# Gate columns carried by the V product, masks and a small product on array groups, and a new order of issue in an attention, gated MLP and expert kernel

## The chip, the cores and the metric

The kernel runs on one core of one Trainium2 chip. The core has a matrix engine (TensorE, PE in the profile; its weight loads are PEld), a vector engine (DVE), a scalar engine (ACT), GpSimd (POOL) and a queue engine (SP) that issues most transfers. Each takes its instructions strictly in the order in which they were written for it, and waits on semaphores for the others. The metric is the time of one execution on the device, in microseconds (us), the median of several runs.

## The reference, cut to what matters

Three stages follow each other, on B=2 sequences of S=768 tokens, 8 heads of 64, so 512 columns a token.

```python
# 1 attention: each chunk of 32 queries sees 8 memory keys and keys c_start-16 .. c_end+8
a = softmax(scale * q_c @ k_full.T);  x = a @ v_full            # -> x (B, S, 512)
# 2 gated MLP
h = gelu(x @ w_in)                                              # 512 -> 1024
u, v = h[..., :512], h[..., 512:]
v_s = einsum('ts,bsd->btd', w_sg, layernorm(v) * g_ln) + b_sg[None, :, None]
x = x + (u * v_s) @ w_out
# 3 experts: 8 of them, one for each token
logits = x @ w_gate;  local = sigmoid(x @ w_local)
e[s] = argmax(logits[s]) if s == 0 or local[s] < 0.5 else e[s-1]
out[s] = softmax(logits[s])[e] * (relu(x[s] @ w1[e]) @ w2[e])   # 512 -> 1024 -> 512
```

## The kernel before, in words

Tokens are worked in 12 tiles of 128 (6 a sequence, `TT`). A product that needs float32 accuracy is made of three passes over operands split into a high and a low part (`PASS`: high x high, high x low, low x high); the split is one ACT or DVE copy (the `_h` tile) and one DVE subtraction (the `_l` tile). The weights `w_in` and `w_out` arrive as 64-bit floats and are rebuilt as float32 on DVE and ACT before their split (class `Conv64`).

For each tile: `Score.mm` makes the scores of 8 heads in two PSUM tiles (`sc`, 4 x 96 columns), each begun by a mask product of all 128 rows that writes all 384 columns (L390); `Attn` takes maximum, exponential and transposes (`nm`, `a`, `at`); `Head` multiplies by v and normalises (`xp`, `rs`, `xt`); `Turn` transposes to `x_h`, `x_l` (`xtp`). `V.s0` (L557) is x times the v half of `w_in`: 12 matmuls of 512 columns into a PSUM tile `vps`; its gelu is ACT Square, DVE, ACT tanh, DVE (`sq`, `th`, `vg`, L538 to L546), then layer norm to `vh`. `U` (L604) is the same with the u half. A gate g multiplies `vh` by `w_sg` (`vsp`, L633) and by `u` and splits to `g_h`, `g_l`. `X1` (L1074) adds g times `w_out` to x and writes the tile to DRAM.

The 16 logits columns (8 experts, local gate, padding) are computed without waiting for the new x: `Logits.x0` (L701, tile `lps`) multiplies the attention's x by the gate weights (`rtxa`, `rtxb`, filled by `rt_fill`, L690 to L692), 48 matmuls of 256 columns for all tokens; `Logits.g0` multiplies g by (w_out times gate weights), a small product that `ConvOut.s4` makes (`wops`, L297). `route1` and what follows make the routing, on small tiles, mostly on DVE; they end with the gathers of the first expert tile (`xg`).

The expert stage (`Moe.run`) takes tiles of 128 tokens of one expert, gathered by GpSimd: `hp` (L1204, L1227), relu to `ht`, `op` (L1268, L1280), scaling on ACT (`o`, L1291) and a scatter by GpSimd (L1292). Its last unit is a pair of tiles that share an expert.

The order is written out by hand. `ORDER` is a table of names; each issues the next piece of its work, and the engines' queues follow from the table (`v04.0`: first stage of V, sequence 0, tile 4; `t011`: transposes; `x12m0`: a quarter of an X1 product; `cv1.1`: conversion of a quarter of the v weights; R and r names: routing; `lx01.0`: logits of x; `lg01.0`: logits of g). PSUM is one pool of 8 banks, most SBUF tiles come from 94 slots of 128 x 512 floats.

Of the kernel before, what the change touches and what calls it, by code (L numbers as in the profile page):

```python
# [25 lines left out]
NE = 8  # L26
NM = 8
# [15 lines left out]
NSLOT = 94  # L43
# [16 lines left out]
t020 lu0 a150.0 cv2.1 p041 s13 t011 q14 lu1 cv2.1 cv2.1 p001 cv2.1 p011 p010 p010 a150.0 p011 p100 a110.2 p011  # L60
a110.2 cv2.1 lu2 t020 t021 p011 cu0.0 t000 p100 p001 cv1.3 lv151 p001 s14 t000 t000 lv101 p100 p100 cu1.0
cv2.2 cv2.3 t001 t001 lv121 t001 cu1.0 cu1.1 a131.0 a140.0 t021 t021 v00.0 cu1.1 a141.0 a150.2 v00.0 cu0.0
p101 v04.0 cu1.1 p101 v00.1 p101 a141.0 a140.0 p101 v00.1 a140.0 a150.2 a131.0 consts2 v00.1 v00.1 v00.1 v03.0
lv131 a141.0 v04.0 lv111 v04.1 lu3 cu3.0 v01.0 a131.0 a140.2 rx lx01.0 cu3.0 v04.1 v04.1 cu1.1 cu2.0 v03.0
cu1.1 v01.0 lx01.1 p121 v01.1 v04.1 v04.1 p111 a140.2 p111 lv110 p110 p111 lx02.0 v00.1 p111 ls8 cu2.0 cu2.1
p110 p121 v01.1 p110 ls6 v00.1 a141.2 a141.2 lo1 v03.1 v03.1 v04.1 lx02.1 a130.0 p110 cu2.1 lv130 a130.0 lv140
v05.0 t100 p121 cu2.1 cs6.0 p121 a130.0 cu3.1 lx00.0 v01.1 t100 a131.2 cu0.1 cu0.1 cu3.1 v04.1 a131.2 v03.1
cu0.1 cu2.1 cu3.1 a130.2 cu1.1 a151.2 ls2 ls0 t101 t100 a130.2 cu0.1 cu1.2 cu1.3 lv120 a151.2 v02.0 lo3 lv141
p120 p131 p130 cu3.1 cu3.1 cu3.1 v04.2 cs2.0 p151 p120 t101 cs8.0 t101 p131 v05.0 p120 p120 cu0.1 p140 lx00.1
v02.0 cu3.2 p141 p131 v01.1 co3.0 cu0.1 cu2.1 cu2.1 cu2.2 cu0.2 p151 ls1 v01.1 v11.0 lv150 p151 v01.1 co3.0  # L70
p151 p141 p131 p130 cu2.3 cs1.0 p130 v01.1 v04.2 v02.1 cu0.3 v11.0 p141 v05.1 cu3.3 p141 v02.1 p130 ls5 cs5.0
# [12 lines left out]
g02.1 g02.1 g02.1 v12.1 co0.2 g03.1 v10.1 v13.1 co2.3 co2.3 v12.1 u11.0 v14.0 v14.0 v12.1 v12.1 u10.0 v12.1
v10.2 v15.0 v15.1 v12.1 v15.1 v15.1 v15.1 u15.0 u15.0 u15.0 v13.1 co0.3 u10.1 v12.1 u15.1 u12.0 x03h0 v13.1
v15.1 u10.1 lx11.0 v14.1 v14.1 co0.4 u11.1 u11.1 v15.1 u15.1 v14.1 v12.2 v10.2 v13.1 u12.0 co0.4 v14.1 u12.0
co3.4 g01.1 u11.1 v14.1 lx11.1 u15.1 x03h1 x03.1 co3.4 v14.1 v14.1 v15.1 v14.2 u10.1 u13.0 u14.0 u14.0 co1.4
co1.4 v13.1 v13.1 v13.1 u14.0 g00.1 u14.1 u12.1 v11.2 u13.0 v13.2 v10.2 x01h0 v14.2 v13.2 u12.1 v15.2 co2.4
co2.4 v15.2 v14.2 x01h1 v12.2 v12.2 v15.2 v11.2 v13.2 lg00.0 u13.0 u13.1 lg02.0 u14.1 u12.1 lg01.0 g12h0 g12h0
g14h0 g12.1 lg01.1 g13h0 g12h1 g13h0 g12h1 lg00.1 lg02.1 r0 g13.1 r0 g14h0 g13h1 u14.1 r0 r1 g12.1 lx12.0  # L90
g14.1 g14h1 r1 r1 r1 r1 r1 g15h0 g15h0 g12.1 g10h0 lx12.1 g10h0 g10.1 r2 g15.1 g14h1 r2 g13h1 g10h1 g10h1
g13.1 r1 g14.1 g15.1 g15.1 g15h1 g10.1 g10.1 x01.1 g15.1 g11h0 g11h0 g14.1 g12.1 zero r4 r5 r5 g14.1 r5 r5 r5
r6 u13.1 u13.1 r6 x03.2 r5 g11h1 g11h1 g10.1 g11.1 g10.1 r2 g15h1 x04h0 x04h1 r6 x02h0 g12.1 g15.1 g15.1 r6 r6
g11.1 g13.1 pre0 pre1 g15.1 r6 g15.1 g13.1 x11m0 pre2 g14.1 g13.1 g11.1 x12m0 x12m1 x11m1 g11.1 g11.1 r7 r1
lg11.0 r5 x04.1 lg10.0 lg10.1 lg11.1 r5 r5 lg12.0 lg12.1 r3 x01.2 r6 x11m2 R1 x02h1 x11m3 R1 R1 R2 R2 R2 R2 R2
R2 pre3 cm0 cm1 x02.1 x05h0 x05h1 x05.1 R3 R3 x10m0 R3 RM RP RP RP RP RP RP RP x12m2 x05.2 x12m3 RA RA x13m0
x13m1 x13m2 RP x13m3 x11.1 x11.2 x10m1 RA RA RA RA RA RA x00h0 x12.1 x13.1 x10m2 x10m3 x00h1 RA RP RP RP RP RP
RA RA x10.1 x15m0 RA RZ x00.1 RP x02.2 x15m1 RP RP RP RP RP RZ R2 RP x12.2 x13.2 RL RP x14m0 x14m1 x15m2 x04.2
x10.2 RP RP RP RP x00.2 R2 x14m2 R4 x14m3 RP RP x14.1 G0 x14.2 RS RT RE RE g15.1 x15m3 x15.1 RT XL RT RT RT
x15.2 XL RS RO cm2 cm3 RP G1 XL XL G2  # L100
# [18 lines left out]
def tile_kernel(  # L119
# [21 lines left out]
    pp = ctx.enter_context(tc.tile_pool(name="pp", bufs=8, space=bass.MemoryType.PSUM))  # L141
# [7 lines left out]


# [8 lines left out]
    mind = [cp.tile([128, 128], BF16, name=f"mind{u}") for u in range(2)]  # L159

    def masks():

        n = 3 * W
        mf = slot([4, n + 128], F32, "amask_f")
        nc.sync.dma_start(mf, amask)
        nc.vector.memset(mrow, 0.0)
        nc.vector.tensor_copy(mrow[:4, :n], mf[:, :n])
        for u in range(2):
            nc.vector.memset(mind[u], 0.0)
            nc.vector.tensor_copy(  # L170
                mind[u][:4].rearrange("p (h q) -> p h q", h=2),
                mf[:, n + 64 * u : n + 64 * u + 64].unsqueeze(1).to_broadcast([4, 2, UQ]),
            )
# [37 lines left out]
    class Conv64:  # L211


        def __init__(self, raws, name, put, n):
            self.raws, self.name, self.put, self.n = raws, name, put, n
# [31 lines left out]
        def s2(self):  # L247
            self.hl = new_split(self.name)
            split_hi(self.hl[0], self.wf, ENG["CH"][self.n])

        def s3(self):
            split_lo(self.hl[1], self.wf, self.hl[0])
            self.put(self.hl)
# [13 lines left out]
    def conv_w_in(raws, kk, half):  # L267
        def put(hl):
            (win_u if half == 0 else win_v)[kk] = hl

        return Conv64(raws, f"in{kk}{half}", put, kk + 4 * (1 - half))

    wgx = cp.tile([128, NP, 16], F32, name="wgx")
    def load_w_out(f):
        return load64(w_out[f * 128 : (f + 1) * 128], 0, f"out{f}")
# [1369 lines left out]
```

## Time and profile before

| what | value |
|---|---|
| median of 3 runs | 422.45 us (421.6 to 423.23) |
| profiled execution | 422.23 us, of which span 420.5 us |
| granted TensorE clock, mean | 0.993 |
| PE / PEld busy | 398.8 us (95%) / 346.9 us (82%) |
| DVE / ACT / POOL busy | 313.6 (75%) / 190.7 (45%) / 43.9 us (10%) |
| memory traffic | 75.95 MB, mean 181 GB/s |

The span is what the profiler saw, 1.7 us less than the execution. Records of matmuls overlap, since they are pipelined and their ends are modelled: what a matmul costs on a full PE is the distance from its start to the next start, not the length of its record. The same holds, less strongly, for DVE and ACT. A stretch in which PE is 10.00 us busy of 10 is one in which it had always something to do.

### The profile page before, as it was taken

How to read it: one execution, taken by the hardware profiler on the slowest of the kernel's cores; microseconds unless marked ns; L12 is line 12 of the kernel's file. 1: busy time of each engine (PE TensorE's matmuls, PEld its weight loads, DVE VectorE, ACT ScalarE, POOL GpSimd, SP SyncE). 2: the span in 40 equal slices, each digit the busy share in tenths (PEclk: the TensorE clock that was granted, in tenths of full speed). 3: DMA queues.
4: the chain of work that ended last, by engine and by line, in shares of the span. 5: the costliest groups of instructions: out<-in, count | busy, mean ns of one | idle time of the engine just before them, and what ended most of it. 6: DMA issues, size and time to landing. Idle time of an engine off the chain costs nothing. (4 is left out here: it accounts for less than half of the span.)

```text
span 420.5 us, 9218 instructions
## 1 busy us (share of the span) xinstructions
PE 398.8 (95%) x3359; PEld 346.9 (82%) x3359; DVE 313.6 (75%) x776; ACT 190.7 (45%) x422; POOL 43.9 (10%) x61
## 2 busy tenths in 40 slices
PE   5799999999999999999999789999999999999991
PEld 3577788899999899999878669989888968958981
DVE  2999989999997988657989997986696455166430
ACT  4898677634331453011030457736484263263420
POOL 1001001030000011000000233000130120110001
PEclk9999999999999999999999999999999999999997
DMA  7999992220100000000565599999699899810001
GB/s 221 372 376 365 311 346 53 77 76 2 51 2 2 0 2 0 2 2 27 172 252 202 169 358 386 393 349 365 180 364 303 299 312 396 311 35 27 20 3 42
DMA packets 43694, 75.95 MB, mean 181 GB/s; under 512 B 5921, under 2 KB 12969, under 8 KB 43642
## 3 DMA queue, kind: packets, MB, share of 16 engines
q1 hardware_dynamic: 39674, 65.40, 45.3%
q0 software_dynamic: 2240, 6.75, 4.4%
q10 hardware_dynamic: 1728, 3.15, 2.0%
q8 instruction: 28, 0.46, 0.5%
q14 instruction: 24, 0.20, 0.1%
HBM read 68.98 MB, written 6.75 MB: 180 GB/s over the span
## 5 line engine op out<-in xcount | busy, mean ns | idle before, releaser
L192 DVE TENSOR_TENSOR we_l<-raw,we_h 128x512 fp32r<-128x512 f32 x128 | 81.1, 688 | 2.1 <-ACT o L1291 0.7
L187 ACT ACTIVATE we_h<-raw 128x512 fp32r<-128x512 f32 x105 | 58.4, 629 | 6.3 <-DVE x L1084 6.3
L1204 PE MATMUL hp<-xe_h,we_h 128*128 128x256 f32 x160 | 45.3, 283 | 0.0
L1204 PE MATMUL hp<-xe_h,we_l 128*128 128x256 f32 x160 | 44.9, 281 | 0.0
L1204 PE MATMUL hp<-xe_l,we_h 128*128 128x256 f32 x160 | 44.8, 280 | 0.0
L1280 PE MATMUL op<-we_h,ht_l 128*128 128x512 f32 x104 | 41.1, 395 | 1.3 <-DVE ht_l L192 1.3
L1280 PE MATMUL op<-we_h,ht_h 128*128 128x512 f32 x104 | 41.7, 401 | 0.1
L1280 PE MATMUL op<-we_l,ht_h 128*128 128x512 f32 x104 | 41.1, 395 | 0.2 <-DVE we_l L192 0.2
L633 PE MATMUL vsp<-sg_h,vh_h 128*128 128x256 f32 x144 | 41.1, 285 | 0.0
L633 PE MATMUL vsp<-sg_l,vh_h 128*128 128x256 f32 x144 | 40.5, 281 | 0.0
L633 PE MATMUL vsp<-sg_h,vh_l 128*128 128x256 f32 x144 | 40.4, 281 | 0.0
L1236 DVE SCALAR_TENSOR_TENSOR ht_l<-hp,ht_h 128x512 fp32r<-128x512 f32 x20 | 13.7, 688 | 28.2 <-ACT ht_h L1235 28.2
L1204 PEld LDWEIGHTS hp<-xe_h,we_h 128*128 128x128 f32 x160 | 30.2, 189 | 0.1
L1204 PEld LDWEIGHTS hp<-xe_l,we_h 128*128 128x128 f32 x160 | 30.1, 188 | 0.0
L1204 PEld LDWEIGHTS hp<-xe_h,we_l 128*128 128x128 f32 x160 | 30.1, 188 | 0.0
L1292 POOL DMA_INDIRECT out_dram<-o,sidx x15 | 15.2, 1011 | 121.9 <-ACT o L1291 102.0
L633 PEld LDWEIGHTS vsp<-sg_h,vh_h 128*128 128x128 f32 x144 | 27.1, 188 | 0.3
L604 PE MATMUL ups<-x_h,in_h 128*128 128x256 f32 x96 | 27.3, 284 | 0.0
L633 PEld LDWEIGHTS vsp<-sg_h,vh_l 128*128 128x128 f32 x144 | 27.1, 188 | 0.0
L633 PEld LDWEIGHTS vsp<-sg_l,vh_h 128*128 128x128 f32 x144 | 27.1, 188 | 0.0
L604 PE MATMUL ups<-x_h,in_l 128*128 128x256 f32 x96 | 27.0, 281 | 0.0
L604 PE MATMUL ups<-x_l,in_h 128*128 128x256 f32 x96 | 26.9, 281 | 0.0
(281 smaller groups left out, 965.7 us busy)
## 6 DMA issues: line engine op xcount, KB each, us to landing
raw<-in_w SPq DMA_DIRECT2D x160, 256.0 KB
v<-in_vw SPq DMA_DIRECT2D x23, 260.0 KB
k<-in_kw SPq DMA_DIRECT2D x24, 192.0 KB
raw_in<-in_w_in SPq DMA_DIRECT2D x16, 256.0 KB
q<-in_qT SPq DMA_DIRECT2D x12, 256.0 KB
x1d<-x ACTq DMA_DIRECT2D x12, 256.0 KB
rsg<-in_w_sgT SPq DMA_DIRECT2D x9, 256.0 KB
raw_out<-in_w_out SPq DMA_DIRECT2D x8, 256.0 KB
```

The source lines that it names most:

```text
L187: nc.scalar.activation(hi, src, AF.Copy)
L192: nc.vector.tensor_tensor(lo, src, hi.bitcast(F32), ALU.subtract)
L604: nc.tensor.matmul(ps[:, i * 256 : (i + 1) * 256], win_u[k][wa][:, f * 128 : (f + 1) * 128], xT[self.b].at(wb, k, 256 * self.g, 256), star ...
L633: nc.tensor.matmul(self.ps[:, h * 256 : (h + 1) * 256], self.vh[s].hl[wa][:, f * 128 : (f + 1) * 128], rhs_sg(wb, s, self.g), start=(s == ...
L1204: nc.tensor.matmul(ps[:, i * 256 : (i + 1) * 256], self.w[f // 4 * 4 + k][wa][:, f % 4 * 128 : (f % 4 + 1) * 128], self.x[k // 2][wb][:, k ...
L1236: nc.vector.scalar_tensor_tensor(l, self.ps[s], 0.0, h.bitcast(F32), ALU.max, ALU.subtract)
L1280: nc.tensor.matmul(self.po[c], h[wa][:, o : o + 128], self.w[8 + k][wb], start=(k == 0 and n == 0), stop=(k == 7 and n == 2),)
L1292: nc.gpsimd.indirect_dma_start(dst, bass.IndirectOffsetOnAxis(ap=sidx[:, c : c + 1], axis=0), o, None, bounds_check=NT * 512 // n - 1, oob ...
```

## The change

- **V carries the gate columns.** The split v weights become 528 wide (8 tiles of a new pool `wv`, the slots fall from 94 to 86); the last 16 columns are the split gate weights (`wide_x`, 8 small DVE instructions). Each of the 12 matmuls of a V becomes two, of 256 and 272 columns, into a PSUM tile of two banks that exists once (`vp`; the other banks fall from 8 to 6). ACT copies the 16 logits columns to `lg`. The 48 matmuls `lps` of x with their ACT copies and DVE fills are gone.
- **w_gate.** The product of w_out and the gate weights has the gate weights (32 columns) stationary and 128 columns moving, on the four column groups of the array, all in one place, with a copy and a transposition behind it.
- **Masks.** The mask product stands behind the scores, uses 4 rows (in the row groups 0 and 32) instead of 128 and writes 64 of each 96 columns.
- **Logits to routing.** DVE adds the two parts in place; two ACT copies go.
- **Last pair.** The second product of the last unit goes tile by tile, and tile 0 is scaled and scattered while tile 1 is multiplied.
- **Order.** The table is new: attention starts with tile 2; the first V stands after fewer tiles' attention; V and U alternate; all gates follow, then the logits of g, all 12 X1 tiles but for their order, and the routing of both sequences.

PE around V. First before, the border between the second and the third V (`vps_1104`, `vps_1166`), with the buffers' numbers:

```order
L557 MATMUL vps_1104<-in31_h_434,x021_h_1066 128x512
L557 MATMUL vps_1104<-in31_l_435,x021_h_1066 128x512
L557 MATMUL vps_1104<-in31_h_434,x021_l_1067 128x512
L557 MATMUL vps_1166<-in01_h_663,x010_h_712 128x512
L557 MATMUL vps_1166<-in01_l_664,x010_h_712 128x512
L557 MATMUL vps_1166<-in01_h_663,x010_l_713 128x512
```

and now, from the end of the second V (`vps_1103`) on, on the same engine:

```order
L599 MATMUL vps_1103<-in31_h_823,x021_l_1057 128x256
L599 MATMUL vps_1103<-in31_h_823,x021_l_1057 128x272
L467 MATMUL at_1137<-ident_79,a141_1049 96x128 x4
L467 MATMUL at_1148<-ident_79,a131_970 96x128 x4
L523 MATMUL xtp_1162<-ident_79,xt02_820 128x128 x2
L523 MATMUL xtp_1162<-ident_79,xt03_1004 128x128 x2
L467 MATMUL at_1172<-ident_79,a151_732 96x128 x4
L467 MATMUL at_1185<-ident_79,a130_1084 96x128 x4
L523 MATMUL xtp_1195<-ident_79,xt02_820 128x128 x2
L523 MATMUL xtp_1195<-ident_79,xt03_1004 128x128 x2
L467 MATMUL at_1203<-ident_79,a100_588 96x128 x4
L494 MATMUL xp_1217<-v110_1101,at110_933 64x65
```

Before, the third V followed the second at once, into another bank. Now transposes of attention weights (`at`) and of x (`xtp`), and eight `xp` that are not shown, stand between the second and the third V.

DVE at the first V. First before (the first two `x_l` are the two halves of the columns of tiles 0 and 1, which the first V waits for; `xt` is the normalised x, `in_l` a split weight):

```order
L192 TENSOR_TENSOR in_l<-w_in_670,in_h 128x512
L465 TENSOR_TENSOR xt_776<-xp,rs 128x256
L192 TENSOR_TENSOR x_l<-xtp,x_h 128x512
L462 RECIPROCAL rs<-rs 128x4
L465 TENSOR_TENSOR xt_977<-xp,rs 128x256
L192 TENSOR_TENSOR in_l<-w_in_827,in_h 128x512
L192 TENSOR_TENSOR x_l<-xtp,x_h 128x512
L233 TENSOR_SCALAR cv_in_1040<-cv_in_1040 128x512
L415 TENSOR_REDUCE nm<-sc 128x4 x2
L192 TENSOR_TENSOR x_l<-xtp,x_h 128x512
```

and now, around the two gelu steps of the first V (`sq`, `vg`):

```order
L582 SCALAR_TENSOR_TENSOR sq<-sq,vps 128x512
L241 TENSOR_SCALAR cv_in_939<-cv_in_939 128x512
L200 TENSOR_TENSOR x_l<-xtp,x_h 128x512
L502 TENSOR_SCALAR rs<-xp 128x4
L587 SCALAR_TENSOR_TENSOR vg<-th,vps 128x512
L457 TENSOR_REDUCE nm<-sc 128x4
L243 TENSOR_SCALAR w_in_1012<-cv_in_939 128x512
L502 TENSOR_SCALAR rs<-xp 128x4
L457 TENSOR_REDUCE nm<-sc 128x4
L200 TENSOR_TENSOR x_l<-xtp,x_h 128x512
L504 RECIPROCAL rs<-rs 128x4
L457 TENSOR_REDUCE nm<-sc 128x4
```

Before, no gelu step stood among DVE's conversions and attention work up to there; now both steps of the first V stand between the splits of x, the normalisation (`rs`) and the maxima (`nm`).

PE at the logits of g. First before, sequence 0, between X1 products, behind the last of the four small products:

```order
L1074 MATMUL x1p<-out_l,g_h 128x512
L1074 MATMUL x1p<-out_h,g_l 128x512
L297 MATMUL wops<-wgx,woTout_2444 128x16 x4
L1074 MATMUL x1p<-out_h,g_h 128x512
L1074 MATMUL x1p<-out_l,g_h 128x512
L1074 MATMUL x1p<-out_h,g_l 128x512
L1074 MATMUL x1p<-out_h,g_h 128x512
L1074 MATMUL x1p<-out_l,g_h 128x512
L1074 MATMUL x1p<-out_h,g_l 128x512
L701 MATMUL lps<-g_h,rtga 128x256
```

and now the small product, between two gate products (the first of its 16 rows):

```order
L678 MATMUL vsp<-sg_l,vh_h 128x256
L678 MATMUL vsp<-sg_h,vh_l 128x256
L319 MATMUL wops<-woTout_2791,wgx 32x128
L319 MATMUL wops<-woTout_2942,wgx 32x128
L319 MATMUL wops<-woTout_2852,wgx 32x128
```

and, behind some more gate products, the logits of sequence 0, behind the last gate product:

```order
L678 MATMUL vsp<-sg_h,vh_h 128x256
L678 MATMUL vsp<-sg_l,vh_h 128x256
L678 MATMUL vsp<-sg_h,vh_l 128x256
L735 MATMUL lps<-g_h,rta 128x256
L735 MATMUL lps<-g_l,rtb 128x256
```

The small product went from four places to one, and the logits of sequence 0 went behind the gates of both sequences.

The core of the diff:

```diff
-NSLOT = 94
+NSLOT = 86
+NWV = 8
+DL = 16
 ORDER = """
-masks lq03 q03 lq02 q02 s03 a031.0 a031.0 a031.0 lq01 a030.0 q01 lv3 s02 a021.0 a030.0 a020.0 lq04 a030.0 s01
+lq02 masks lq01 q02 s02 consts1 a021.0 q01 s01 a021.0 a021.0 a021.2 a020.0 a020.0 a020.0 a020.2 lq04 q04 s04
...
-    pp = ctx.enter_context(tc.tile_pool(name="pp", bufs=8, space=bass.MemoryType.PSUM))
+    wv = ctx.enter_context(tc.tile_pool(name="wv", bufs=NWV))
+    pp = ctx.enter_context(tc.tile_pool(name="pp", bufs=6, space=bass.MemoryType.PSUM))
+    vp = ctx.enter_context(tc.tile_pool(name="vp", bufs=1, space=bass.MemoryType.PSUM))
...
+    def bank2(name):
+        return vp.tile([128, 1024], F32, tag="d", name=name)
+    def wide(name):
+        return [wv.tile([128, 512 + DL], F32R, tag="w", name=f"{name}_{x}") for x in "hl"]
...
+    def wide_x(k):
+        h, l = (t[:, 512:] for t in win_v[k])
+        nc.vector.tensor_copy(h, wgx[:, k, :DL])
+        nc.vector.tensor_tensor(l, wgx[:, k, :DL], h.bitcast(F32), ALU.subtract)
...
-            for c in range(4):
-                nc.tensor.matmul(ps, self.t[:, c, :], wgx[:, c, :], start=(c == 0), stop=(c == 3))
-            yield
-            rt_fill("g", self.f, ps)
+    def w_gate():
+        ps = bank([128, 128], "wops")
+        for c in range(4):
+            for f in range(4):
+                nc.tensor.matmul(
+                    ps[32 * f : 32 * f + 32], wgx[:, c, :], turned[f][:, c, :], start=(c == 0), stop=(c == 3)
+                )
...
-            for u in range(2):
-                nc.tensor.matmul(
-                    self.sc[u], mind[u], mrow[:, v * W : (v + 1) * W].unsqueeze(1).to_broadcast([128, 4, W]),
-                    start=True, stop=False,
-                )
...
+            for u in range(2):
+                p = slice(32 * u, 32 * u + 4)
+                nc.tensor.matmul(
+                    part(self.sc[u]),
+                    mind[p], part(mrow[p, v * W : (v + 1) * W].unsqueeze(1).to_broadcast([4, 4, W])),
+                    start=False, stop=True,
+                )
...
         def s0(self):
-            ps = bank([128, 512], "vps")
+            ps = bank2("vps")
...
-                    nc.tensor.matmul(
-                        ps, xT[self.b].at(wa, k, self.tt * 128, 128), win_v[k][wb],
-                        start=(n == 0), stop=(n == 11),
-                    )
+                    for o0, o1 in ((0, 256), (256, 512 + DL)):
+                        nc.tensor.matmul(
+                            ps[:, 256 + o0 : 256 + o1],
+                            xT[self.b].at(wa, k, self.tt * 128, 128), win_v[k][wb][:, o0:o1],
+                            start=(n == 0), stop=(n == 11),
+                        )
...
             self.g = Gelu()
-            self.g.s0(ps)
+            self.g.s0(ps[:, 256:768])
+            yield
+            nc.scalar.activation(lg[:, self.b * TT + self.tt, :], ps[:, 768 : 768 + DL], AF.Copy)
...
-        def x0(self, i):
-            self.ps[i] = bank([128, 256], "lps")
-            logits_mm(self.ps[i], "x", xT[self.b], 256 * i, 256)
...
-        lo = tp.tile([128, TT, 16], F32, tag="r_lo", name="r_lo")
-        nc.scalar.copy(lo, ps[:, :, 16:32])
+        nc.vector.tensor_tensor(L, ps[:, :, 16:32], L, ALU.add)
         yield
-        nc.vector.tensor_tensor(L, ps[:, :, 0:16], lo, ALU.add)
+        nc.vector.tensor_tensor(L, ps[:, :, 0:16], L, ALU.add)
...
-                h, l = self.ht[s] = new_split("ht")
+                h, l = self.ht[s] = wide_split("ht")
...
             half, i = divmod(s, len(self.cols))
+            if self.last:
+                i, half = divmod(s, 2)
...
                         o.l2(s)
+                        if o.last and s == 1:
+                            o.out(0)
...
-            outs(T[-1])
+            if T[-1].last:
+                T[-1].out(1)
+            else:
+                outs(T[-1])
```

## Rows read from the trace of the kernel before

**Rows 1.** Windows of 10 us: busy us and instructions of each engine, clock, DMA, GB/s.

```profile
20.00:30.00 10.00, 8.93 (x167) 7.06 (x165) 9.79 (x30) 9.76 (x36) 0.00 (x0) 1.00 1.06 377
...
40.00:50.00 10.00, 9.49 (x149) 7.64 (x149) 9.72 (x30) 7.15 (x17) 0.00 (x0) 1.00 1.03 300
...
100.00:110.00 10.00, 10.00 (x87) 10.00 (x86) 9.44 (x21) 2.24 (x5) 0.00 (x0) 1.00 0.14 44
...
230.00:240.00 10.00, 7.83 (x67) 6.39 (x66) 9.59 (x43) 3.13 (x7) 1.43 (x2) 1.00 0.40 133
240.00:250.00 10.00, 8.68 (x41) 6.83 (x42) 9.90 (x17) 6.59 (x13) 5.16 (x5) 1.00 0.96 332
```

**Rows 2.** Timeline of PE, 45 to 48 us: start, us, line, operation, names.

```profile
45.60 0.49 PE L390 MATMUL sc<-mrow,mind 128*128 128x384 bf16 x2
46.02 0.89 PE L398 MATMUL sc<-k,q 64*64 64x96 f32 x32
...
47.26 0.48 PE L557 MATMUL vps<-in_h,x_h 128*128 128x512 f32 x1
...
48.04 0.40 PE L557 MATMUL vps<-in_h,x_h 128*128 128x512 f32 x1
48.27 0.39 PE L557 MATMUL vps<-in_l,x_h 128*128 128x512 f32 x1
```

**Rows 3.** The tile lps: duration min/median/max in ns, first and last start.

```profile
L701 PE MATMUL lps<-x_h,rtxa x24: 274/280/386, 60.1 to 182.4; 128*128 128x256 f32 x24
```

**Rows 4.** Timeline of PE around the small product wops and around a column-group product.

```profile
161.65 0.96 PE L297 MATMUL wops<-wgx,woTout 128*128 128x16 f32 x8
162.46 0.36 PE L604 MATMUL ups<-x_h,in_h 128*128 128x256 f32 x1
...
398.50 1.96 PE L1268 MATMUL op<-raw,ht 128*32 128x128 f32 x64
400.39 0.50 PE L1280 MATMUL op<-we_h,ht_h 128*128 128x512 f32 x1
```

**Rows 5.** Timeline of DVE, 45 to 58 us: start, us, line, operation, names.

```profile
45.88 0.42 DVE L465 TENSOR_TENSOR xt<-xp,rs 128x256 f32<-128x256 f32 x1
...
49.64 0.55 DVE L415 TENSOR_REDUCE nm<-sc 128x4 f32<-128x384 f32 x1
50.10 0.68 DVE L192 TENSOR_TENSOR x_l<-xtp,x_h 128x512 fp32r<-128x512 f32 x1
50.70 0.41 DVE L235 TENSOR_SCALAR w_in<-cv_in 128x512 uint32<-128x512 uint32 x1
51.03 0.55 DVE L415 TENSOR_REDUCE nm<-sc 128x4 f32<-128x384 f32 x1
...
54.55 0.67 DVE L546 SCALAR_TENSOR_TENSOR vg<-th,vps 128x512 f32<-128x512 f32 x1
...
57.02 0.17 DVE L690 CAST rtxa<-wgx 128x16 fp32r<-128x16 f32 x1
...
57.39 0.17 DVE L690 CAST rtxa<-wgx 128x16 fp32r<-128x16 f32 x1
```

**Rows 6.** Timeline of ACT at the first V's gelu.

```profile
50.33 0.60 ACT L538 ACTIVATE sq<-vps 128x512 f32<-128x512 f32 x1 [1.33 <-PE vps L557]
```

**Rows 7.** Waits of PE behind the gates: us in total, times, longest.

```profile
PE hp L1227 <- ACT xe_h L187: 1.3, 1, 1.3
...
PE inv L976 <- DVE s_eqj L957: 0.8, 1, 0.8
```

**Rows 8.** Timeline of POOL at the end.

```profile
409.99 0.98 POOL L1292 DMA_INDIRECT out_dram<-o,sidx  x1 [7.67 <-ACT o L1291]
413.48 0.98 POOL L1292 DMA_INDIRECT out_dram<-o,sidx  x1 [2.51 <-ACT o L1291]
```

**Rows 9.** Timeline of ACT at the end.

```profile
409.03 0.69 ACT L1291 ACTIVATE o<-op,psl 128x512 f32<-128x512 f32 x1 [8.00 <-PE op L1280]
411.87 0.69 ACT L1291 ACTIVATE o<-op,psl 128x512 f32<-128x512 f32 x1 [2.15 <-PEq L1557]
```

More of the change, by code (lines that the diff above doesn't have):

```diff
@@ L211, in tile_kernel, with __init__ @@
     class Conv64:
-        def __init__(self, raws, name, put, n):
-            self.raws, self.name, self.put, self.n = raws, name, put, n
+        def __init__(self, raws, name, put, n, new=None):
+            self.raws, self.name, self.put, self.n, self.new = raws, name, put, n, new
         def s0(self):
@@ L341, in rhs_sg, with wide_split @@
         return wsg_s[s // 2][w][:, (s % 2) * 256 : (s % 2) * 256 + 256]
+    def wide_split(name):
+        return tuple(t[:, :512] for t in wide(name))
     class Tr:
@@ L399, in mm @@
                             self.sc[u][hs, j, :], self.q[us_, h4, j, :], self.k[h4][us_, j, :],
-                            start=False, stop=(j == 3),
+                            start=(j == 0), stop=False,
                         )
+            for u in range(2):
+                p = slice(32 * u, 32 * u + 4)
[4 more added lines that the diff above has]
+                )
     class Attn:
@@ L700, in logits_mm @@
             for w in range(2):
[L701 removed]
+                nc.tensor.matmul(ps, RT[w][:, k, :], src.at(w, k, t0, n), start=(i == 0), stop=(i == 7))
                 i += 1
@@ L1273, in l2 @@
             half, i = divmod(s, len(self.cols))
+            if self.last:
+                i, half = divmod(s, 2)
             c = self.cols[i]
             if half == part[0] == 0:
-                self.po[c] = bank([128, 512], "op")
+                if self.two and not self.last:
+                    if i == 0:
+                        self.po2 = bank2("op")
+                    self.po[c] = self.po2[:, i * 512 : i * 512 + 512]
+                else:
+                    self.po[c] = bank([128, 512], "op")
             for k in range(4 * half + part[0], 4 * half + part[1]):
@@ L1307, in __init__ @@
             self.T = [Unit(u) for u in units]
+            self.T[-1].last = self.T[-1].two
             n = len(units)
@@ L1406, in run @@
                     for s in range(M):
-                        feed(o, 8 + s * 2 // M * 4, 2 if o.two and s % 2 else 0)
+                        if o.last:
+                            feed(o, 8 + s % 2 * 4, 0)
+                        else:
+                            feed(o, 8 + s * 2 // M * 4, 2 if o.two and s % 2 else 0)
                         if s == 0 and t:
@@ L1475, in tile_kernel @@
     at("zero", zero_row)
-    at("rx", lambda: [rt_fill("x", k, wgx[:, k]) for k in range(NP)])
-    for kind, n, ns in (("v", 4, 4), ("u", 4, 4), ("o", 4, 5), ("s", 9, 2)):
+    at("lw", load_wg)
+    for k in range(NP):
+        at(f"rx{k}", wide_x, k)
+    at("rz", rt_zero)
+    at("cw", w_gate)
+    for kind, n, ns in (("v", 4, 4), ("u", 4, 4), ("o", 4, 4), ("s", 9, 2)):
         for i in range(n):
@@ L1517, in tile_kernel @@
         at(f"pre{i}", moe.pre, 4 * i + 4)
-    for i, n in enumerate((2, 4, 5, 8)):
-        at(f"cm{i}", moe.conv_to, n, "act")
+    for i in range(8):
+        at(f"cm{i}", moe.conv_to, i + 1, "act")
     for name, fn, *a in (
@@ L1524, in tile_kernel @@
         ("G0", moe.T[0].gather, True), ("G1", moe.T[1].gather), ("G2", moe.T[2].gather),
-        ("XL", lambda: (yield from moe.T[0].xt_late([x.t for x in xs[1][TT - LATE :]]))),
+        ("XL", lambda: (yield from moe.T[0].xt_late(xs[1][TT - LATE :]))),
     ):
```

220 lines of the change are left out of this document (110 added, 110 removed).

## The prediction, made before the changed kernel ran

> **What bounds the kernel now.** I read the windows of 10 us first. In all 18 windows from 50 to 230 us, and in nearly all from 250 to 400 us, PE is 10.00 us busy of 10; the one shown holds 87 matmuls of 256 columns [rows 1]. There DVE, at 9.44, is nearly as full and yet PE waits for nothing, so the end moves by what PE's queue gains or loses. In two stretches PE waits. Up to 50 us DVE is full (9.79 and 9.72 of 10) and PE's records cover idle array time, since few of its instructions are long: there the end moves by what DVE must do before the first V products. And between 230 and 250 us, where routing hands over to the experts, PE lacks 2.17 and 1.32 us [rows 1], of which the waits name 0.8 (`inv`) and 1.3 (`hp`) [rows 7]. The chain of waits holds only the last transfer. TensorE's granted clock is 1.00 in all these windows, its 2.4 GHz level, so none of it is priced by the clock.
>
> Prices are distances of starts, not records. A 256-column matmul is 10/87 = 0.115 us [rows 1], one of 512 columns 48.27 - 48.04 = 0.23 [rows 2], though their records last 0.28 [rows 3] and 0.40 [rows 2]. On DVE, from the starts between 49.64 and 51.03 [rows 5]: `nm` 0.46, a 512-wide subtraction 0.60, a 512-wide shift or clamp 0.33; three 16-column fills take 57.39 - 57.02 = 0.37, so 0.12 each.
>
> **The change part by part.**
>
> *Logits of x.* 48 matmuls `lps` of 256 columns (24 as in [rows 3], 24 for the low half) go, between 60 and 183 us, where PE is full: 48 x 0.115 = -5.5 us. I see nothing that could hide this. The six ACT copies and twelve DVE fills that go with them cost no PE time.
>
> *V in two parts.* 144 matmuls of 512 columns become 288. By columns a pair costs 0.115 + 0.115 x 272/256 = 0.237 against 0.231 (two times 0.115): 144 x 0.006 = +0.9 us. The bounds: 0, if the added columns hide; and above, if a split matmul paid the whole excess of records, 2 x 0.28 - 0.40 = 0.16, 144 x 0.16 = +23 us, for which the cadence 0.115 to 0.23 leaves no room, as two short ones take exactly one long one. I take +0.9.
>
> Here one rule speaks against the change. Two 256-column matmuls take the time of one of 512 in the rows, so no fixed cost for each instruction shows at this size [rows 1, 2]. The Trainium skill, TensorEngine Tiling (Array Packing), Instruction Overhead, has about 60 cycles of overhead for each matmul. If that came on top of the columns, 144 more matmuls at 60/2.4 GHz = 25 ns (an estimate by that page) would cost 3.6 us, and the sum below would be 3.6 us higher; the same section's other statement, that one column takes as long as 60, makes it a floor, which 256 columns never meet, and the trace agrees with the floor.
>
> *w_gate.* Four groups of 8 records cost 162.46 - 161.65 = 0.81 us each [rows 4], 3.2 together. The new product has 16 matmuls of 128 columns on a group of 32 array columns, which appear as two records each. The nearest row has 64 such records in 400.39 - 398.50 = 1.9 us, 0.03 each [rows 4]: 32 x 0.03 = 1.0, plus a transposition, put at the price of a 256-column matmul, 0.115. So -2.1 us, in full windows; bounds 0 and -2.3. The copy between it and the transposition lies beside gate products that stand between them in PE's order.
>
> *Masks.* A pair costs 46.02 - 45.60 = 0.42 us [rows 2], twelve 5.0. Two thirds of the columns, and two row groups that may run beside each other: between 0.11 and 0.28 a pair. I take 0.21, so -2.5 in all (bounds -1.7 to -3.7). All of it lies before 60 us, where DVE decides, so it counts only in the next sum.
>
> *The early order.* Before, the first V starts at 47.26 [rows 2], held by the `xt` at 45.88 [rows 5], whose transposes precede it. In the new order the tightest place of this kind that I find by adding such prices along both queues is the `xt` that the third V's transposes need. Up to it DVE has more to do than up to the old place: 4 `nm` (1.8), 4 more shifts and clamps (1.3), `sq` and `vg` of the first V (1.3), one more `in_l` and one more `x_l` (1.2), 8 fills (1.0), less one `x_h` copy and small things (0.7): +5.9 us. In that time PE has also issued more: two V (24 pairs x 0.237 = 5.7) and eight `at` (0.9, each put at a 256-column price), less four `xtp` (0.4), eight `xp` (0.5, an estimate of half that price) and the masks (2.5): +3.2. What follows on PE can thus end 5.9 - 3.2 = 2.7 us later than its own work says. Bounds: 0, if the old idle time of DVE before that place shrinks as much, and +6 if the gelu steps that now stand in DVE's queue make it wait as long again. I take +2.7. The one V tile is part of this. Before, the second to fourth V followed each other at once; now each V waits until the last reader of the one before, `vg`, and the ACT copy of the logits have gone. Behind a waiting V stand in PE's queue the U products, transposes and `xp`, for which DVE and ACT then wait in turn.
>
> *Transfers.* Up to 60 us the queues are full (377 GB/s, [rows 1]). Counted along SP's queue, the last v weight stands behind 9.1 MB now and behind 11.0 MB before; the last keys behind 13.1 MB in both. The gate weights come earlier (32 KB) and the mask twice (6.5 KB each), behind the first q. I take 0, with some tenths to either side.
>
> *Routing.* The routing of sequence 0 lay under gates; now it follows the last gate with that of sequence 1, and as cover come all twelve X1 instead of the last few. Summed along the queues with the prices above (estimates), PE has some 45 us of work from its last gate to the first `hp`, DVE some 31; before 28 and 25. So the 0.8 us at `inv` and the small gaps around it should close; the wait of `hp` (1.3) hangs on a gather, transposes and a split that stay: -0.8. Bounds -2 and +3, the latter if the last X1 writes, which now end later in the order, hold up the first gather. The two in-place additions on DVE for an ACT copy are below 0.3 us and covered by X1.
>
> *Last pair.* The last `o` ends at 411.87 + 0.69 = 412.56 [rows 9], but its scatter starts at 413.48, behind the one issued at 409.99 [rows 8]. If tile 0's is issued some 5 us earlier, the last starts 0.27 after `o`, as the first of the two does: 412.83, so -0.65 (bounds 0 and -0.7). Its splits are due after 12 matmuls instead of 24; they lie ready before `op` starts, as PE goes on at once [rows 4].
>
> *Experts.* Slots: 86 + 8 = 94 as before, with the pair's `ht` in the wide tiles. PE is full there and issues the same: 0.
>
> The sum: PE's work up to the experts changes by -5.5 + 0.9 - 2.1 - 2.5 = -9.2; early order +2.7, routing -0.8, tail -0.65: -7.95. From the profiled execution, 422.23 us (its span and 1.7 around it), that is 414.3, and the median of before lies 0.22 above that execution, so 414.5.
>
> **The rivals.**
>
> *The one V tile decides (slower).* Between consecutive V's PE has 2.8, 3.7, 3.2, 3.2, 3.3 us of other work for the first five gaps, then 6.1, 4.7 and four times 5.7 (estimates, the same prices along the new order). Before, the first V's Square started at 50.33 [rows 6] and its `vg` ended at 54.55 + 0.67 = 55.22 [rows 5], 4.9 us, since DVE had queued other things between the steps. If the chain from a V's last matmul to the end of `vg` takes 5.8 us, the first five gaps are short by 3.0, 2.1, 2.6, 2.6 and 2.5, the seventh by 1.1 and the last four by 0.1 each: 14.3 us instead of the 2.7 above, so 414.5 + 11.6 = 426.1. From a chain of 5.3 us on the kernel is slower than before, from 5.6 by more than can be told from no change. For it: DVE is full just there. Against it: the new order puts only three short rows between `sq` and `vg`, so 0.6 + 0.6 + 0.6 + 0.7 with hand-overs is near 3.3; and all later gaps but one exceed 4.9.
>
> *The early stretch takes more.* DVE stays behind up to the fourth or fifth V (+6 instead of +2.7) and the gather of the first expert tile waits (+1 instead of -0.8): 419.6. For it: DVE at 9.7 of 10 has no reserve, so what it loses there it wins back only under the gates. Against it: no V but the first five stands so close behind another.
>
> *Each added matmul has a fixed cost.* The records of `wops`, of 16 columns, start 0.81/8 = 0.10 apart [rows 4], while 16 columns at 0.115 for 256 would take 0.007; so 0.09 of a short matmul isn't its columns. Were a quarter of that on top of each of the 144 added ones (all of it, 13 us, is excluded by [rows 1, 2]), V would cost 3.3 us more: 417.8. Against it: two short ones take what a long one takes. The estimate by the page named above comes out 0.3 us higher.
>
> *More than expected.* DVE's idle time in the first 46 us shrinks with the new order, and the small gaps at routing vanish: 414.5 - 2.7 - 1.2 = 410.6.
>
> **How the numbers follow.** The forecast has 0.56, its own range 411 to 418; the V tile 0.13, the early stretch 0.14, the fixed cost 0.07, the larger gain 0.10. The range 409.5 to 421 takes in all but most of the V tile's case and the tail of the larger gain. About 0.5% (2.1 us) can be told from no change in this kernel. Faster: the forecast, the larger gain, the fixed cost and 0.09 of the early stretch, 0.82; same: the rest of the early stretch, 0.05, and 0.03 of the V tile with a chain near 5.3 us, 0.08; slower 0.10.
>
> **What would show it.** In the changed profile: no `lps` before the last gate; `vps` starts 0.115 and 0.122 apart; `wops` near 1 us in one place; PE at 10.00 in the windows after some 55 us, and waits of PE on DVE `vg` below 1 us each; the first `hp` near 232 us instead of 239.8, with `inv` not waited for; from there to the end as many us as before, less 0.65 at the last scatter. I am wrong if PE shows waits on `vg` or on the logits' copy of over 1 us in most V's, if windows between 50 and 110 us fall below 9.5, or if the first `hp` stands after 237.

## The result and the profile after

The changed kernel took 416.53 us (415.53 to 417.23, 4 runs) against 422.84 us (421.6 to 423.25, 4 runs) of the kernel before: a ratio of 0.9854, 95% interval 0.9823 to 0.9885. Three later measurements of the same kernel, each beside the kernel before on one chip, gave 0.9802 (0.9783 to 0.9821), 0.9867 (0.9840 to 0.9895) and 0.9813 (0.9784 to 0.9842). By the medians it is 5.7 to 8.1 us faster; the forecast was 414.5, 8 us below the median of before.

The profiled execution took 417.23 us, span 415.4 us, mean granted clock 0.985. Windows of 10 us, columns as in [rows 1] (after span and length: PE, PEld, DVE, ACT, POOL busy with instructions, clock, DMA share, GB/s):

```profile
20.00:30.00 10.00, 10.00 (x156) 7.86 (x158) 8.58 (x25) 8.59 (x31) 0.00 (x0) 0.66 1.01 359
...
40.00:50.00 10.00, 10.00 (x173) 8.41 (x174) 9.42 (x35) 8.65 (x26) 0.85 (x2) 1.00 0.95 313
...
200.00:210.00 10.00, 9.55 (x82) 6.95 (x83) 9.34 (x31) 2.53 (x7) 0.00 (x0) 1.00 0.08 29
...
230.00:240.00 10.00, 9.30 (x64) 7.83 (x64) 8.61 (x22) 4.95 (x9) 4.34 (x5) 1.00 0.51 168
240.00:250.00 10.00, 8.33 (x45) 5.89 (x44) 6.66 (x11) 4.33 (x8) 0.40 (x1) 1.00 0.98 347
```

From 40 to 200 us PE has 9.98 or more in every window; before, the first of these had 9.49 [rows 1]. The hand-over between 230 and 250 us lacks 0.70 and 1.67 us instead of 2.17 and 1.32. A gap is new: 0.45 us from 200 to 210 us, where before PE was full:

```profile
200.00:210.00 10.00, 10.00 (x56) 8.66 (x55) 9.55 (x28) 0.55 (x2) 0.00 (x0) 1.00 0.50 171
```

And one number is new: a granted clock of 0.66 from 20 to 30 us. In windows of 1 us:

```profile
18.00:19.00 1.00, 0.76 (x4) 0.43 (x4) 1.00 (x4) 1.00 (x5) 0.00 (x0) 1.00 0.90 289
19.00:20.00 1.00, 0.72 (x8) 0.34 (x11) 1.00 (x3) 1.00 (x4) 0.00 (x0) 1.00 0.74 205
...
21.00:22.00 1.00, 1.00 (x10) 0.62 (x8) 0.74 (x2) 1.00 (x4) 0.00 (x0) 0.50 0.95 338
...
27.00:28.00 1.00, 1.00 (x19) 0.64 (x21) 1.00 (x4) 0.74 (x2) 0.00 (x0) 0.60 1.05 376
```

PE's clock falls to 0.50, the 1.2 GHz level, from 21.0 to 27.8 us. Ahead of that PE had waited: 0.72 to 0.88 of each us busy from 17 to 20 us.

V's matmuls on PE, timeline (start, us, line, operation, names; x2 is one pair of 256 and 272 columns):

```profile
127.27 0.41 PE L599 MATMUL vps<-in_l,x_h 128*128 128x256 f32 x2
127.51 0.41 PE L599 MATMUL vps<-in_h,x_l 128*128 128x256 f32 x2
127.76 0.41 PE L599 MATMUL vps<-in_h,x_h 128*128 128x256 f32 x2
```

A pair takes 0.244 us from start to start, the median of all twelve V products; 512 columns took 0.23 [rows 2], more exactly 0.232 by the same median. And 256 columns took 0.118 from start to start already before, 2.01 us for 17 steps here:

```profile
99.91 0.28 PE L633 MATMUL vsp<-sg_l,vh_h 128*128 128x256 f32 x1
...
101.92 0.28 PE L633 MATMUL vsp<-sg_h,vh_h 128*128 128x256 f32 x1
```

The mask pair, on PE after, is now 0.21 us against 0.42 [rows 2] (0.32 in four places in the first 24 us):

```profile
15.46 0.28 PE L439 MATMUL sc<-mrow,mind 4*128 4x256 bf16 x2
15.67 0.64 PE L467 MATMUL at<-ident,a 128*96 128x128 f32 x4
```

The small product takes 179.76 - 178.75 = 1.0 us in one place; four times 0.81 before [rows 4]:

```profile
178.75 1.08 PE L319 MATMUL wops<-woTout,wgx 128*32 128x128 f32 x32
179.76 0.39 PE L678 MATMUL vsp<-sg_h,vh_h 128*128 128x256 f32 x1
```

The tile `lps` (duration min/median/max, first and last start) is left with the logits of g alone, all behind the last gate; the rows of x [rows 3] are gone:

```profile
L735 PE MATMUL lps<-g_h,rta x24: 276/280/386, 184.2 to 196.0; 128*128 128x256 f32 x24
```

The first expert products, on PE, first before and then after:

```profile
239.84 0.50 PE L1227 MATMUL hp<-we_h,xe_h 128*128 128x512 f32 x1 [1.34 <-ACT xe_h L187]
```

```profile
234.47 0.50 PE L1253 MATMUL hp<-we_h,xe_h 128*128 128x512 f32 x1 [0.30 <-ACT xe_h L195]
...
242.28 0.50 PE L1313 MATMUL op<-we_h,ht_h 128*128 128x512 f32 x1 [1.54 <-ACT ht_h L195]
```

The first `hp` starts at 234.47 instead of 239.84 us. The waits of PE (total, times, longest), to be held against [rows 7]; first one of before that stands beside those, then after:

```profile
PE op L1280 <- DVE ht_l L192: 1.3, 1, 1.3
```

```profile
PE op L1313 <- ACT ht_h L195: 1.5, 1, 1.5
...
PE xgp L1188 <- DMA xg<-x1d,gidx: 0.4, 1, 0.4
...
PE hp L1253 <- ACT xe_h L195: 0.3, 1, 0.3
PE rps L789 <- DVE r_gn L779: 0.3, 1, 0.3
...
PE pre L859 <- ACT r_row L795: 0.2, 1, 0.2
```

`inv` is no longer waited for, `hp` 0.3 instead of 1.3. New are 0.4 for a gather and 0.3 and 0.2 at two small products of routing (`rps`, `pre`; the gap from 200 to 210 us). At the first `op` products PE waited before as well, 1.3 us for `ht_l`, and now 1.5 for `ht_h`. At the end, PE's last matmul, POOL and then ACT, against [rows 8, 9]; PE before comes first:

```profile
411.38 0.39 PE L1280 MATMUL op<-we_h,ht_l 128*128 128x512 f32 x1
```

```profile
407.02 0.39 PE L1313 MATMUL op<-we_h,ht_l 128*128 128x512 f32 x1
```

```profile
402.86 0.98 POOL L1325 DMA_INDIRECT out_dram<-o,sidx  x1 [5.15 <-ACT o L1324]
408.41 0.98 POOL L1325 DMA_INDIRECT out_dram<-o,sidx  x1 [4.57 <-ACT o L1324]
```

```profile
407.45 0.69 ACT L1324 ACTIVATE o<-op,psl 128x512 f32<-128x512 f32 x1 [4.86 <-PE op L1313]
```

The last scatter starts 0.27 us behind its scaling, 407.45 + 0.69 = 408.14, and no longer behind the one before it. It follows the start of PE's last matmul, at 407.02, by 1.39 us; before it was 413.48 - 411.38 = 2.10.

### The profile page after: what moved, and what is told of

Read it like the earlier page. It is cut to its first block, busy times and chain, and to the rows that moved or that the text cites. A ratio compares the mean times of both kernels' runs of the same rounds, so it can differ in the third digit from the quotient of the medians.

```text
span 415.4 us, 9403 instructions
## 1 busy us (share of the span) xinstructions
PE 397.6 (96%) x3456; PEld 350.4 (84%) x3456; DVE 312.2 (75%) x757; ACT 193.0 (46%) x433; POOL 42.4 (10%) x60
```

## The experiments

Times are medians; where a kernel is compared with the changed one, both ran side by side on the same chip unless said otherwise.

**The changed kernel again** (no edit).

> The changed kernel once more, unchanged, for a second profile. In the first one TensorE's granted clock was 0.50 from 21 to 27.6 us, and PE's lag behind its own work was 21.2 us at 60 us against 17.4 before. Theory A (DVE holds the early stretch): without that low clock the lag at 60 us is still 20 to 21, since DVE was full there anyway; time 415.5 to 416.5. Rival B (the clock made the lag): without it the lag falls to 17.5 to 18.5 and the run to about 413.5. If the clock falls again at the same place, it belongs to the kernel.

Measured 414.42 us (413.71 to 415.53), ratio 0.9802. From its profile, a window and the first `hp`:

```profile
20.00:30.00 10.00, 9.36 (x189) 6.99 (x182) 9.69 (x30) 9.94 (x35) 0.00 (x0) 1.00 1.03 364
```

```profile
232.81 0.50 PE L1253 MATMUL hp<-we_h,xe_h 128*128 128x512 f32 x1 [0.30 <-ACT xe_h L195]
```

The clock did not fall before the last matmul. The first V starts at 41.63 us (43.36 in the first profile), the first `hp` at 232.81 (234.47). Where the 1.7 us come from shows on DVE, in the first profile and then in the second:

```profile
19.79 0.41 DVE L250 SCALAR_TENSOR_TENSOR w_in<-raw_in,w_in 128x256 uint32<-128x256 uint32 x1
...
29.42 0.16 DVE L502 TENSOR_SCALAR rs<-xp 128x4 f32<-128x4 f32 x1 [0.61 <-PE xp L494]
```

```profile
19.64 0.41 DVE L250 SCALAR_TENSOR_TENSOR w_in<-raw_in,w_in 128x256 uint32<-128x256 uint32 x1
...
27.70 0.16 DVE L502 TENSOR_SCALAR rs<-xp 128x4 f32<-128x4 f32 x1
```

The two profiles are 0.15 us apart ahead of the fall and 1.72 at its end, and in the first DVE waits for PE in between. So the fall cost some 1.6 us in that execution, for good, of the 3.4 us that half speed for 6.8 us takes from PE. DVE stays full (9.69 of 10). The time lies between the two theories, 1.1 us below A's range and 0.9 above B's number, and neither is right alone: of the 3.8 us (21.2 - 17.4) by which PE's lag had grown, 1.7 went with the clock and some 2.1 stayed.

**Masks as before, in the changed kernel** (shortened; the loading of the mask rows goes back with it).

```diff
-            for j in range(4): ... scores, start=(j == 0)
-            for u in range(2): ... mask on 4 rows, 64 of 96 columns, stop=True
+            for u in range(2): ... mask on 128 rows, 96 columns, start=True
+            for j in range(4): ... scores, stop=(j == 3)
```

> The changed kernel with the masks as before: first in each score tile, all 128 rows, 384 columns. It puts 12 x (0.42 - 0.21) = 2.5 us of PE work back, all before 60 us. Theory A (DVE holds the early stretch, so PE's work there lies beside DVE's): 0 to +1 us against the changed kernel. Rival B (PE's queue sets the time also there): +2.5 us.

Measured 414.67 us (413.77 to 415.58) beside 414.42: +0.25, within both intervals. 2.5 us of PE work put back before 60 us cost nothing that can be told in the time: theory A. In the one profiled execution the first `hp` stands at 234.10, 1.3 later than in the profile beside it, but still among the places that the changed kernel itself shows.

**Last pair as before, in the changed kernel.**

```diff
-            self.T[-1].last = self.T[-1].two
+            self.T[-1].last = False
```

> The changed kernel with the last pair's second product as before (half by half, both scatters at the end). Theory A: the last scatter waits again for the transfer of the one before, +0.65 to +0.7 us, all behind the last matmul. Rival B: tile by tile the splits are due earlier and PE loses some of it again, so that the difference is below 0.3.

Measured 418.11 us (417.79 to 419.13): +3.7, and neither theory had that. PE's last matmul, ACT and POOL at the end:

```profile
405.50 0.40 PE L1313 MATMUL op<-we_h,ht_l 128*128 128x512 f32 x1
```

```profile
405.98 1.27 ACT L1324 ACTIVATE o<-op,psl 128x512 f32<-128x512 f32 x2 [11.00 <-PEq L1601]
```

```profile
406.94 0.98 POOL L1325 DMA_INDIRECT out_dram<-o,sidx  x1 [10.70 <-ACT o L1324]
410.40 0.98 POOL L1325 DMA_INDIRECT out_dram<-o,sidx  x1 [2.47 <-issue]
```

Both scalings now start together behind the last matmul. In the kernel before, with the same order but a bank for each result, they stood 2.8 us apart [rows 9]; in the changed one a pair's two results share the one two-bank tile, unless it is the last pair. 405.50 (the start of the last matmul) to 410.40, the last scatter, is 4.9 us against 1.39. The changed kernel's exception for its last pair removes not only the 0.7 us of before but also 2.8 us that its own two-bank tile would have added.

This kernel is the changed one up to its last unit, and its profile has no fall of the clock before 408 us. Yet its first V starts at 43.44 and its first `hp` at 234.40, as late as in the first profile. Among DVE's waits here is one for a transfer of raw weights:

```profile
26.24 0.29 DVE L232 TENSOR_SCALAR cv_in<-raw_in 128x256 uint32<-128x256 uint32 x1 [0.96 <-DMA raw_in<-in_w_in]
```

So the clock is not the only thing that moves the early stretch from one execution to the next: the third profile of the changed kernel has this wait too (0.9), the first, second and fourth do not. No experiment changed the transfers.

**V in 512 and 16 columns.**

```diff
-                    for o0, o1 in ((0, 256), (256, 512 + DL)):
+                    for o0, o1 in ((0, 512), (512, 512 + DL)):
```

> The changed kernel with each V pass cut into 512 and 16 columns instead of 256 and 272: the same work by columns. Theory A (price by columns): a 16-column matmul takes under 0.01, so the time is the same within 1 us. Rival B (a short matmul has a price of its own, as the 16-column records of the small product before, 0.10 apart): 144 x (0.23 + 0.10 - 0.237) = +13 us. The page's floor of 60 cycles, 0.025, gives 144 x (0.23 + 0.025 - 0.237) = +2.6.

Measured 428.64 us (427.52 to 431.23), +14.2 over the changed kernel: 14.2/144 = 0.10 us more for each pair. On PE, and PE's weight loads:

```profile
102.73 0.48 PE L599 MATMUL vps<-in_l,x_h 128*128 128x512 f32 x2
103.07 0.48 PE L599 MATMUL vps<-in_h,x_l 128*128 128x512 f32 x2
```

```profile
102.47 0.19 PEld L599 LDWEIGHTS vps<-in_h,x_h 128*128 128x128 f32 x1
102.71 0.30 PEld L599 LDWEIGHTS vps<-in_l,x_h 128*128 128x128 f32 x2
```

A pair takes 0.34, so 0.11 for 16 columns. Theory B: a short matmul has a price of its own. The Trainium skill, TensorEngine Tiling (Array Packing), Instruction Overhead, has about 60 cycles of overhead for each matmul, with one column as long as 60; at 2.4 GHz that is 0.025 us, an estimate. The trace shows four times that here, 0.10 to 0.11. Cut in the middle, both halves take little more than those 16 columns (256 columns: 0.118), and that is why carrying the gate columns costs little. What the 0.11 consists of was not separated: each of the two pieces loads its weights itself, and two such loads also start 0.11 us apart (0.30 for the two, 0.19 for one), so it may be the price of the load and not of the matmul.

**The logits of x twice, in the kernel before.**

```diff
-            logits_mm(self.ps[i], "x", xT[self.b], 256 * i, 256)
+            for _ in range(2):
+                logits_mm(self.ps[i], "x", xT[self.b], 256 * i, 256)
```

> The kernel before with the 48 logits matmuls of x issued twice, the second time from the start again, so that the result is the same. Theory A (PE full, each 256-column matmul is worth its distance of starts): 48 x 0.115 = +5.5 us. Rival B (they lay in gaps or beside DVE's work): 0 to +2 us; then the gain of the change came from elsewhere.

Measured 428.75 us against 423.17: ratio 1.0148 (1.0107 to 1.0189), so +4.5 to +8.0 us. Theory A, by an interval that shuts out B.

**V in two ordinary banks** (shortened; with it the pairs of experts get a bank for each result again).

```diff
-            ps = bank2("vps")
+            pa, pb = bank([128, 512], "vps"), bank([128, 512], "vpt")
...
+            for i, p in enumerate(self.ps): ... Square and both DVE steps, 256 columns each
```

> The changed kernel with each V in two ordinary banks of a pool of 8 in place of the one two-bank tile, so that no V waits for the gelu of the one before; the gelu reads the two banks with two instructions instead of one, which adds 1 ACT and 2 DVE instructions to each V. Theory A (the single tile costs next to nothing; PE's waits for it sum to 0.2 us in the trace): the same within 0.7 us, or slower by the added instructions, up to +1.5. Rival B (the single tile makes the early lag): faster by 1 to 2.7 us.

Measured 415.58 us (414.98 to 418.51), ratio 0.9845 (0.9796 to 0.9893). The changed kernel was not measured beside it; its ratios elsewhere are 0.980 to 0.987. So no gain shows, but by the times alone one of about 1 us can't be excluded. In its profile the first V starts at 41.84 and the first `hp` at 233.19, among the changed kernel's (41.63 to 43.36, 232.81 to 234.47): the single tile isn't what holds the early stretch.

**Six more subtractions on DVE.**

```diff
             split_lo(hl[1], psf, hl[0])
+            if self.b == 0:
+                split_lo(hl[1], psf, hl[0])
```

> The changed kernel with the splits of x of sequence 0 (the x_l subtraction, 0.60 us on DVE) done twice, six times before 65 us: 3.6 us more of DVE, of which 2.4 stand before the third V. Theory A (DVE holds the early stretch): +2.4 to +3.6 us. Rival B (transfers, ACT or PE hold it): 0 to +0.7 us.

Measured 420.75 us (417.34 to 423.85, 10 runs; 420.40 without the longest, ratio 0.9925, 0.9888 to 0.9963). The executions fall apart by clock: the four at 0.994 to 0.996 took 417.34, 417.41, 417.60 and 419.81, the others, at 0.977 to 0.990, 420.4 us and more. The former are, but for one, 3.0 us above the changed kernel's 414.4, as theory A has it. That one was measured on another chip, but the kernel with q on POOL (below), measured beside this one, also took 414.40. The rest goes with the clock. The profile's windows, in an execution of 0.986, and its first added subtractions:

```profile
20.00:30.00 10.00, 8.52 (x146) 6.33 (x139) 8.62 (x25) 8.28 (x29) 0.00 (x0) 0.84 0.98 340
30.00:40.00 10.00, 8.97 (x157) 7.36 (x156) 8.11 (x26) 7.25 (x21) 0.00 (x0) 0.87 0.98 319
```

```profile
36.27 2.74 DVE L200 TENSOR_TENSOR x_l<-xtp,x_h 128x512 fp32r<-128x512 f32 x4 [0.22 <-ACT x_h L195]
```

0.84 and 0.87 here, and PE at 8.5 to 9.0 of 10. But both falls, from 19.0 and from 29.3 us, come before the first added subtraction, at 36.27 (x4: two splits, each done twice). So the added work cannot have brought them.

**q scaled on POOL** (shortened).

```diff
-            nc.scalar.activation(self.q, self.q, AF.Copy, scale=1.0 / math.sqrt(D))
+            nc.gpsimd.tensor_scalar(self.q, self.q, 1.0 / math.sqrt(D), None, ALU.mult)   # 9 of 12
```

> The changed kernel with nine of the twelve scalings of q on POOL, which is idle in the first 60 us, instead of ACT: some 4.5 us less of ACT before 50 us, where ACT is 9.9 of 10 busy from 20 to 40 us. Theory A (DVE alone holds the early stretch): 0 to +1 us. Rival B (ACT holds it together with DVE): -1 to -2 us. If POOL takes far longer than ACT's 0.5 us, scores come late and it is slower by 1 us or more.

Measured 414.40 us (414.07 to 415.47), ratio 0.9791 (0.9758 to 0.9824): the same as the changed kernel at its best. The changed kernel was not measured beside it, and against its other ratios, up to 0.987, the times alone leave room for Rival B's gain. The profile speaks against it: the first V starts at 42.89 and the first `hp` at 233.37, no earlier than in the changed kernel, so 4.5 us less of ACT did not shorten the early stretch.

**The changed kernel a third time, and the clamps on POOL.**

```diff
-            nc.vector.tensor_scalar(mag, mag, F64_LO, F64_HI, ALU.max, ALU.min)
+            (nc.gpsimd if self.n < 8 else nc.vector).tensor_scalar(mag, mag, F64_LO, F64_HI, ALU.max, ALU.min)
```

> The changed kernel unchanged, as the measure beside the next kernel: 414 to 416.5 us. Both theories expect executions with a granted clock near 0.995 at the lower end and those near 0.985 some 1.7 us above.

> The changed kernel with the clamp of the eight converted w_in tiles (512 columns, 0.33 us each on DVE) on POOL, which is idle there: 2.6 us less of DVE before 60 us, the counterpart of the doubled splits. Theory A (DVE holds the early stretch, about 1 us for each us of its work before the third V): -1 to -2.5 us, and a version faster than the changed kernel. Rival B (POOL takes several times DVE's 0.33 us, or slows DVE beside it, so that the weights come late): 0 to +3 us.

Measured 417.38 (416.05 to 419.12) and 417.81 us (415.7 to 420.58). The line of the clamp, by engine, and a wait of DVE:

```profile
L241 POOL TENSOR_SCALAR cv_in<-cv_in x8: 1916/1918/2227, 15.7 to 61.7; 128x512 f32<-128x512 f32 x8
...
L241 DVE TENSOR_SCALAR cv_out<-cv_out x4: 394/421/427, 99.5 to 146.3; 128x512 f32<-128x512 f32 x4
```

```profile
DVE w_in L243 <- POOL cv_in L241: 4.0, 4, 1.2
```

POOL takes 1.92 us for what DVE does in a record of 0.42, and DVE waits 4.0 us for it, more than the 2.6 us that it was spared. The times fall into Rival B's range and there is no better version: 415.70 and 416.22 at clocks of 0.996 and 0.995, where the changed kernel beside it has 416.08 at 0.996. The profiled execution, at 0.984, also has the clock at 0.50 from 39.8 us for 10.2 us. What less work on DVE would gain is thus not shown.

**The changed kernel a fourth time, and the old masks again.**

> The changed kernel unchanged, beside the next. Its executions so far lie between 413.7 and 419.1 us with granted clocks of 0.984 to 0.996, those of the kernel before between 0.992 and 0.996. Theory A (in the early stretch PE is so thinly filled that its clock falls to 1.2 GHz in some executions, and this spreads the times): again some executions below 0.992, each 1.5 to 3 us above those at 0.996. Rival B (the spread is the chip's alone): no tie between clock and time.

> The changed kernel with the masks as before, again: 2.5 us more of PE work before 60 us, which lie beside DVE's. In its first run all five executions had a clock of 0.995 or more. Theory A (more PE work in the early stretch keeps the clock up): all or nearly all at 0.995 again, median 1 to 3 us below the changed kernel's where that one's clock falls, and equal to it (within 0.7) where it doesn't. Rival B (the masks have nothing to do with it): the same spread as the changed kernel, median 0 to 1 us above.

Measured 416.07 (413.96 to 417.46) and 415.99 us (414.61 to 418.15). The clocks of the old masks were 0.992 to 0.996 this time: its earlier row of high clocks was chance, and the masks don't hold the clock up. Of the 20 executions of the changed kernel, the five below 0.990 have a median of 417.5 us, the fifteen others 416.0; one of the five, with 414.42, is among the fastest. The tie is there, but weak. The mean also holds the end behind the last matmul, where the clock is low in every profile: the pair as before has 0.989 from that alone. The kernel before had no execution below 0.991.

The profiles say where the clock fell before the end. Of the four of the changed kernel only the first has it in the early stretch. The third has no fall there. The fourth has one of 3.4 us, from 242.9 us, at the hand-over to the experts.

## Why the prediction was right

The time lies in the range and 2.0 us above the forecast, a quarter of the forecast gain; in the later measurements 0.1 us below it, 2.9 above and 1.6 above.

- *Logits of x, -5.5*: the rows are gone, and doubling them costs 4.5 to 8.0. Right.
- *V in two parts, +0.9*: mis-sized. A pair takes 0.244, not 0.237, and one of 512 columns took 0.232: 144 x 0.012 = +1.7. The price of 0.115 for 256 columns was too low, since 10/87 counts the records that reach over the window's two edges. From start to start it was 0.118 in the kernel before too, and at that price a pair of 256 and 272 columns is 0.243. So two short matmuls do not take exactly one long one, but 0.236 against 0.232. The full fixed-cost rival (3.3 us above) was not met, a quarter of it was.
- *w_gate, -2.1*: 1.0 and a transposition instead of 3.2. Right.
- *Masks, -2.5, hidden*: 0.21 a pair as taken, and hidden, by both mask experiments (+0.25 and -0.08).
- *Early order, +2.7, and routing, -0.8*: PE's work before the first `hp` changed by -5.5 + 1.7 - 2.1 - 2.5 = -8.4, and `hp` came 5.4 us earlier in the first profile, 7.0 in the second. So both together gave back 3.0 and 1.4 instead of 1.9. The first has the clock's fall in it, some 1.6 us, which no step of mine had. Routing came out near its -0.8 partly by luck: `inv` is not waited for any more, as said (-0.8), but the wait of `hp`, which was to stay, fell by 1.0, and `rps`, `pre` and the gather took back 0.9. With these -0.9 the early order gave back some 2.3 in the second profile. That DVE's work counts in that stretch is shown by the doubled subtractions (+3.0 us for 3.6 us of work); PE's masks and ACT's scalings of q, put back or taken away there, did not move it. That DVE alone holds it is not shown: transfers held it up in some executions.
- *Experts, 0*: off by +1.0 us in the first profile, but not by a fixed cost. From the first `hp` to the last matmul it was 411.38 - 239.84 = 171.54 us, and now 407.02 - 234.47 = 172.55; the other profiles have 405.33 - 232.81 = 172.52, 172.98, and 174.45 with the clock's fall in it. But kernels with the same expert code have less: 171.22 and 173.16 in the two profiles of the old masks, which are one program, 171.58 with q on POOL, 171.10 with the doubled subtractions. So the new hand-over does not by itself cost 1 us. Part of the difference lies at the first `op`, where PE waited 1.5 to 2.1 us for `ht_h` in the longer profiles, but for the second, and 0.5 to 0.7 (for `ht_l`) in the shorter ones. What decides between the two stays open.
- *Last pair, -0.65*: -0.7, and for a second reason, which only the experiment brought up.

Together, for the second profile (415.53 us): -8.4 + 1.4 + 1.0 - 0.7 = -6.7, and 422.23 - 6.7 = 415.5. This balances by construction, as three of the terms are read from the two profiles. The rival of the one V tile fell. Two banks for each V show no gain, and of all that waited for the tile in the first profile (us, times) PE's weight loads have this line:

```profile
  PEld vps L599: 0.2, 1
```

## What to carry to other kernels

Where the matrix engine is full, columns appended to a product that runs anyway replace a whole product, if no piece falls into the range in which a matmul has a price by itself: cut in the middle. Work removed where another engine holds the pace is worth nothing. Executions of one program can differ by a us or two, in the clock and in who waits where, so a term of 1 us is not read from two profiles. A shared result tile ties together the readers of its halves: look for who waits on the whole.

## What the runs showed that I had not expected

- The granted clock fell to 0.50 in some executions of the same program and not in others: for 6.8 us in the first profile, where that cost some 1.6 us, for 3.4 us at another place in the fourth. What brings it is not shown.
- 16 columns cost 0.10 to 0.11 us here, nearly as much as 256 (0.118).
- POOL's clamp of 128 x 512 floats took 1.92 us, DVE's 0.42.
